# Attention and two feed-forward layers on one core: the first layer's hidden chunks are handled two at a time in one PSUM bank

## The chip, the cores and the metric

One core of a Trainium2 chip runs the whole program. The metric is the device time of one execution in microseconds (us). The kernel before was run three times: 1081.27, 1083.11 and 1083.59 us, median 1083.11 us.

## The reference, cut to what matters

```python
# 4 batches, 8 heads, 576 positions, head size 64
scores = q @ k.T / 8 + (cum[:, :, :, None] - cum[:, :, None, :])   # cum: running sum of log f
attn = softmax(where(causal, -1e9, scores)) @ v
x = attn as 2304 tokens x 512
h = x @ w_in                    # 512 -> 2048
g = h * clip(h + 3, 0, 6) / 6   # first layer
x = g @ w_out                   # 2048 -> 512
h = x @ w2_in                   # second layer, other weights
g = where(h >= 1, h, where(h <= -1, 0, (h + 1)**2 / 4))
out = g @ w2_out
```

## The kernel before

Tokens are the free axis. The first layer goes over nine blocks of 256 tokens (`NB`, `T`), the second over blocks of 512, 512, 512, 512 and 256 (`T2`). The 2048 hidden features are cut into 16 chunks of 128 (`NCH`). One entry of `steps` is one block and one chunk, (j, n, c): 144 entries for the first layer, 80 for the second. Each product of two fp32 numbers is made of three matmuls, since every operand is held as a rounded part and a rest: high by high, low by high, high by low.

`moe_h(g)` makes the features of one entry: 12 matmuls (4 slices of 128 inputs, 3 each) into one PSUM bank `hp`. In the first layer these have 256 columns. Then come four elementwise instructions on 256 columns: ScalarE (ACT) Relu out of `hp` into `u` (L567), VectorE (DVE) minimum and product with `hp` (L568), ACT rounding of `u` into the high half of `g` (helper L121), DVE subtraction into its low half (helper L129). `moe_o(g)` multiplies `g` with the second weights: 12 matmuls that add to the block's accumulators. In the first layer these are two banks, each holding two slices of 256 columns (L608); since two slices share a bank, a block begins with two matmuls of a zero row, one per bank, that set the bank to zero (L601). In the second layer the matmuls have 512 columns, three in a row for each group of 128 tokens (L615), with (weight part a, feature part bb) in the order (0,0), (1,0), (0,1).

Order of the work. The main loop takes one entry g per turn: weights due for g (`weights_until`), `moe_h(g)`, attention pieces, `moe_o(g - 2)` (`LAG` is 2), attention pieces again. Attention pieces (scores, softmax, transposes, products with v) are taken from a list `seq`, so many at each point that running costs meet a goal (`goal`, `due`). They share TensorE (PE), ACT, DVE and the four PSUM banks of `ps` (later two more) with the first layer, and are all done by entry 112 (`g7`). In the first 32 entries blocks 0 and 1 alternate, block 1 being `STAG` = 9 chunks behind. Weights live in 12 slots of 8 KB per partition (16 from entry 112 on). `plan_weights` decides which chunk sits where, and counts a slot as free `LAG` + 1 entries after its last use. The tile framework then sets the final order on each engine by a simulated schedule, so an engine's instructions need not come in the order in which the loop writes them. All loads are issued from SyncE's queue (SP), each in its turn.

Of the kernel before, what the change touches and what calls it, by code (L numbers as in the profile page):

```python
# [8 lines left out]
F32 = mybir.dt.float32  # L9
F32R = mybir.dt.float32r  # L10
I32 = mybir.dt.int32
AF = mybir.ActivationFunctionType
# [4 lines left out]
P = 128  # L17
NCH = DFF // P
KD = DM // P
T = 256  # L20
# [16 lines left out]

SLOTS = 12
MORE = 16 - SLOTS
LAG = 2  # L40
STAG = 9
XT = 11
PRE0, PRE1 = 38, 106
WRAW = 4
# [30 lines left out]
def tile_kernel(  # L75
# [38 lines left out]
    ncum = dram.tile([B * H, S], F32, name="ncum")  # L114
    wsb = [wpool.tile([P, 2, 8, P], F32R, name=f"w{s}") for s in range(SLOTS)]
    ident = const.tile([P, P], F32, name="ident")
    zero = const.tile([1, P], F32R, name="zero")

    def rounded(eng, out, in_):
        if eng == "a":  # L120
# [9 lines left out]


    steps = []
    for i in range(NCH + STAG):
        if i < NCH:
            steps.append((0, i, i))
        if i >= STAG:
            steps.append((1, i - STAG, i - STAG))
    for j in range(2, NB2):
        order = range(NCH) if j % 2 else range(NCH - 1, -1, -1)
        for n, c in enumerate(order):  # L140
# [58 lines left out]
    def w_keep(c, s):  # L199
        nc.sync.dma_start(out=wf[c], in_=wsb[s].bitcast(F32))  # L200
# [339 lines left out]
    def moe_x(j):  # L540

        t0, w = sum(T2[:j - NB]), T2[j - NB]
        for k in range(KD):
            x = ext.tile([P, 2, T2[0]], F32R, tag=f"x2{k}", name=f"x2{k}", bufs=2)
            hi, lo = x[:, 0, 0:w], x[:, 1, 0:w]
            nc.sync.dma_start(out=lo.bitcast(F32), in_=x2d[k * P:(k + 1) * P, t0:t0 + w])
            rounded("p", hi, lo.bitcast(F32))
            rest("v", lo, lo.bitcast(F32), hi)
            xt[j, k] = x

    def moe_h(g):
        j, n, c = steps[g]
        layer = int(j >= NB)
        w = T2[j - NB] if layer else T
        ws = wsb[where[g]]
        hp = bank("hp")
        hp = hp[:, 0:w]
        for k in range(KD):
            x = xt[j, k]
            for a, bb in ((0, 0), (1, 0), (0, 1)):  # L560
                nc.tensor.matmul(  # L561
                    hp, lhsT=ws[:, a, k], rhs=x[:, bb, 0:w], start=(k == 0 and a == 0 and bb == 0),
                    stop=(k == KD - 1 and bb == 1),
                )
        u = ffn.tile([P, T2[0] if layer else T], F32, tag="u", name="u", bufs=2)[:, 0:w]
        if layer == 0:
            nc.scalar.activation(out=u, in_=hp, func=AF.Relu, bias=3.0, scale=1.0)  # L567
            nc.vector.scalar_tensor_tensor(out=u, in0=u, scalar=6.0, in1=hp, op0=ALU.min, op1=ALU.mult)  # L568
        else:
            nc.scalar.activation(out=u, in_=hp, func=AF.Relu, bias=0.5, scale=0.5)  # L570
            nc.scalar.activation(out=u, in_=u, func=AF.Square)  # L571
            nc.vector.scalar_tensor_tensor(out=u, in0=hp, scalar=1.0, in1=u, op0=ALU.max, op1=ALU.min)  # L572
        gg = ffn.tile([P, 2, T2[0] if layer else T], F32R, tag="g", name="g", bufs=3)[:, :, 0:w]
        rounded("a", gg[:, 0], u)
        rest("v", gg[:, 1], u, gg[:, 0])
        gt[g] = gg
# [10 lines left out]
    def moe_o(g):  # L587
        j, n, c = steps[g]
        layer = int(j >= NB)
        t0 = sum(T2[:j - NB]) if layer else j * T  # L590
        ws = wsb[where[g]]
        gg = gt.pop(g)
        if n == 0:
            acc[j] = [(ps_x if j == 1 else ps_o).tile([P, 512], F32, tag=f"o{k}", name=f"o{k}") for k in range(2)]
            if layer:
                acc[j] += [ps_b[0].tile([P, 512], F32, tag="ps", name="ps") for _ in range(T2[j - NB] // P - 2)]
        if layer == 0:

            if n == 0:
                for k in range(2):  # L600
                    nc.tensor.matmul(  # L601
                        acc[j][k].rearrange("p (a n) -> p a n", a=4), lhsT=zero,
                        rhs=zero.unsqueeze(1).to_broadcast([1, 4, P]), start=True, stop=False,
                    )
            for k in range(KD):
                o = acc[j][k // 2][:, k % 2 * T:k % 2 * T + T]
                for a, bb in ((0, 0), (1, 0), (0, 1)):
                    nc.tensor.matmul(  # L608
                        o, lhsT=ws[:, a, KD + k], rhs=gg[:, bb], start=False,
                        stop=(n == NCH - 1 and bb == 1 and k % 2 == 1),  # L610
                    )
        else:
            for k in range(len(acc[j])):
                for a, bb in ((0, 0), (1, 0), (0, 1)):
                    nc.tensor.matmul(  # L615
                        acc[j][k], lhsT=gg[:, bb, k * P:(k + 1) * P],
                        rhs=ws[:, a, KD:2 * KD].rearrange("p k n -> p (k n)"),
                        start=(n == 0 and a == 0 and bb == 0), stop=(n == NCH - 1 and bb == 1),
                    )
# [104 lines left out]
    nc.vector.tensor_scalar(out=lf0, in0=lf0, scalar1=-8.0, scalar2=None, op0=ALU.mult)  # L724
    nc.sync.dma_start(out=lf, in_=f.rearrange("b h (g l) -> (b h g) l", g=SEG))
    make_identity(nc, ident)
    zf = att.tile([P, P], F32, tag="prob0", name="zf")
    nc.vector.memset(zf[0:1], 0.0)
    nc.vector.tensor_copy(zero, zf[0:1])
    logs(lf)  # L730
    seq, ends = attention_pieces()
    u_load(0)
# [22 lines left out]
        weights_until(-1)  # L755


    spans = [(0, STAG, 1), (STAG, 2 * NCH, 2)] + [(j * NCH, (j + 1) * NCH, j + 1) for j in range(2, NB)]
    cost = [sum(x[0] for x in seq[:n]) for n in range(len(seq) + 1)]
    due = [ends[group(min(j, NB - 1))] for _, _, j in spans]  # L760
    goal, n0 = [], pos
# [10 lines left out]
            n0 += 1  # L772

    ext = None
    for g in range(len(steps) + LAG):
        if g == g7:
            assert pos == len(seq)
            att_cm.__exit__(None, None, None)
            ext = ctx.enter_context(tc.tile_pool(name="ext", bufs=2, reuse_waits="tile"))
            wsb += [ext.tile([P, 2, 8, P], F32R, name=f"w{s}", bufs=1) for s in range(SLOTS, SLOTS + MORE)]  # L780
        weights_until(g)
        if g < n1:
            for part in range(2):
                if part == 0:
                    moe_h(g)
                elif g >= LAG:
                    moe_o(g - LAG)
                    j, n, c = steps[g - LAG]
                    if j == 0 and again[c]:
                        w_keep(c, where[g - LAG])  # L790
                while pos < len(seq) and cost[pos] < goal[2 * g + part] - 1:
                    seq[pos][1]()
                    pos += 1
            if g == 2 * NCH + LAG - 1:
                psx_cm.__exit__(None, None, None)
                ps_b.append(ctx.enter_context(
                    tc.tile_pool(name="ps_b", bufs=2, space=bass.MemoryType.PSUM, reuse_waits="tile")
                ))
            if g == g7 + 20:
                moe_x(NB)  # L800
            if g == n1 - 1:
                moe1_cm.__exit__(None, None, None)
                ffn = ctx.enter_context(tc.tile_pool(name="moe2", bufs=2, side="right", reuse_waits="tile"))
        else:
            second[0] = True
            if g < len(steps):
                j, n, c = steps[g]
                moe_h(g)
                if n == 4 and j + 1 < NB2:
                    moe_x(j + 1)  # L810
            moe_o(g - LAG)


# [36 lines left out]
```

## Time and profile before

| | |
|---|---|
| runs | 1081.27, 1083.11, 1083.59 us |
| profiled execution: span from first to last instruction | 1083.4 us |
| PE busy | 1034.3 us, 95% |
| PE weight loads busy | 903.9 us, 83% |
| DVE busy | 591.8 us, 55% |
| ACT busy | 541.5 us, 50% |
| matmuls | 6556 |

The page gives no time for the profiled execution other than its span, which lies inside the three runs. Busy PE is modelled from pipelined matmuls, so its share is not a share of peak; the starts of successive matmuls tell the pace.

### The profile page before, as it was taken

The numbers are of one execution on the slowest core, as the hardware profiler recorded it, in microseconds if no ns is written. First come the engines' busy times: TensorE is split into PE (matmuls) and PEld (weight loads), VectorE is DVE, ScalarE is ACT, GpSimd is POOL, SyncE is SP. The second block draws the span as 40 slices with busy tenths as digits, with TensorE's granted clock in tenths as the row PEclk, the third lists the DMA queues.
The fourth block names the chain that finished last, engine by engine and source line by source line (L and its number), as shares of the span: only waits on it lengthen the run. The fifth ranks groups of instructions, "written<-read, shape, count | busy, mean of one in ns | idle before, by whom it ended". The sixth has DMA issues, their size and how long they took to land.

```text
span 1083.4 us, 18101 instructions
## 1 busy us (share of the span) xinstructions
PE 1034.3 (95%) x6556; PEld 903.9 (83%) x6556; DVE 591.8 (55%) x1510; ACT 541.5 (50%) x1330; POOL 89.8 (8%) x223
## 2 busy tenths in 40 slices
PE   7987999989799989999999999999999999999998
PEld 5776989979688889888989999888888888888887
DVE  7999984766577776777653436422422322332232
ACT  6877755656456655556553235533333333333343
POOL 2200010111021111121101000000100100000000
PEclk8688999999999999999999999999999999999999
DMA  8976681783586686864826035200200200010010
GB/s 235 337 222 185 213 299 54 226 277 111 182 282 197 202 298 185 282 212 123 249 68 253 2 96 167 90 1 1 77 1 1 72 6 1 19 39 1 1 40 20
DMA packets 69785, 144.20 MB, mean 133 GB/s; under 512 B 11584, under 2 KB 38720, under 8 KB 65600
## 3 DMA queue, kind: packets, MB, share of 16 engines
q1 hardware_dynamic: 67136, 134.66, 39.6%
q0 software_dynamic: 2560, 8.39, 2.0%
q8 instruction: 51, 0.84, 0.3%
q14 instruction: 38, 0.31, 0.1%
HBM read 116.74 MB, written 26.29 MB: 132 GB/s over the span
## 4 chain that ended last, share of the span: by engine, by line
PE 69%; DMA 15%; DVE 7%; issue 4%; ACT 4%; SPq 1%; POOL 0%; DVEq 0%; ACTq 0%; POOLq 0%
PE hp L561 31%; PE o L608 12%; PE o L615 10%; PE ps L615 8%; DMA qraw<-in_q 5%; DMA dec<-ncum 3%; PE pt L432 3%; DMA kraw<-in_k 2%; PE av L474 2%; DMA wraw<-in_w 2%; PE sc L388 1%; DMA x2d<-osb 1%; DMA wf<-wr 1%; DVE prob L339 1%; DVE wr L186 1%
## 5 line engine op out<-in xcount | busy, mean ns | idle before, releaser
L608 PE MATMUL o<-g,w 128*128 128x256 f32 x1728 | 250.3, 289 | 16.8 <-ACT g L121 15.3
L561 PE MATMUL hp<-xt,w 128*128 128x256 f32 x1728 | 250.6, 292 | 7.8 <-ACT w L121 5.1
L608 PEld LDWEIGHTS o<-g,w 128*128 128x128 f32 x1728 | 225.9, 191 | 26.7 <-ACT g L121 19.2
L561 PEld LDWEIGHTS hp<-xt,w 128*128 128x128 f32 x1728 | 226.8, 194 | 14.5 <-ACT w L121 6.1
L561 PE MATMUL hp<-x,w 128*128 128x512 f32 (+1 forms) x960 | 211.4, 369 | 0.0
L561 PEld LDWEIGHTS hp<-x,w 128*128 128x128 f32 x960 | 169.1, 188 | 32.5
L572 DVE SCALAR_TENSOR_TENSOR u<-hp,u 128x512 f32<-128x512 f32 (+1 forms) x80 | 50.8, 637 | 195.9 <-ACT u L571 195.9
L129 DVE TENSOR_TENSOR g<-u,g 128x256 fp32r<-128x256 f32 (+1 forms) x224 | 112.8, 505 | 71.5 <-ACT g L121 71.1
L121 ACT ACTIVATE g<-u 128x256 fp32r<-128x256 f32 (+1 forms) x224 | 106.1, 475 | 88.4 <-DVE u L572 55.3
L570 ACT ACTIVATE u<-hp 128x512 f32<-128x512 f32 (+1 forms) x80 | 44.6, 557 | 173.3 <-PE hp L561 171.5
L615 PE MATMUL o<-w,g 128*128 128x512 f32 x480 | 125.0, 396 | 0.0
L615 PEld LDWEIGHTS o<-w,g 128*128 128x128 f32 x480 | 89.1, 188 | 19.9
L345 ACT ACTIVATE prob<-prob,mx 128x512 f32<-128x512 f32 (+4 forms) x144 | 83.5, 581 | 37.4 <-DVE mx L339 37.0
L615 PE MATMUL ps<-w,g 128*128 128x512 f32 x384 | 100.4, 396 | 0.0
L568 DVE SCALAR_TENSOR_TENSOR u<-u,hp 128x256 f32<-128x256 f32 x144 | 59.4, 416 | 53.8 <-ACT u L567 53.2
L567 ACT ACTIVATE u<-hp 128x256 f32<-128x256 f32 x144 | 53.8, 378 | 67.2 <-PE hp L561 65.4
L615 PEld LDWEIGHTS ps<-w,g 128*128 128x128 f32 x384 | 72.3, 188 | 17.4
L432 PE MATMUL pt<-ident,prob 128*128 128x128 f32 (+1 forms) x400 | 69.1, 296 | 12.6 <-DVE prob L417 12.1
L339 DVE CUSTOM_DVE_ANT_0 prob<-sc,dec 128x256 f32<-128x256 f32 (+1 forms) x112 | 58.8, 533 | 25.1 <-PE sc L388 11.9
L121 ACT ACTIVATE pt<-pt 128x512 f32<-128x512 f32 (+3 forms) x160 | 61.9, 433 | 18.7 <-PE pt L432 18.2
L432 PEld LDWEIGHTS pt<-ident,prob 128*128 128x128 f32 (+1 forms) x400 | 50.3, 150 | 18.4 <-DVE prob L417 12.8
L178 ACT ACTIVATE wr<-wraw 128x512 f32<-128x512 f32 x64 | 43.0, 671 | 44.5 <-DMA wf<-wr 19.0
(76 smaller groups left out, 975.5 us busy)
## 6 DMA issues: line engine op xcount, KB each, us to landing
wraw<-in_w SPq DMA_DIRECT2D x64, 512.0 KB, 6.4
w<-wf SPq DMA_DIRECT2D x24, 1024.0 KB, 8.5
dec<-ncum SPq DMA_DIRECT2D x45, 256.0 KB, 6.6
kraw<-in_k SPq DMA_DIRECT2D x64, 144.0 KB, 3.8
wf<-w SPq DMA_DIRECT2D x8, 1024.0 KB
wf<-wr POOLq DMA_DIRECT2D x32, 256.0 KB, 6.0
w<-wf SPq DMA_DIRECT2D x16, 512.0 KB, 4.1
vv<-in_v SPq DMA_DIRECT2D x16, 320.0 KB, 10.6
```

The source lines that it names most:

```text
L121: nc.scalar.activation(out=out, in_=in_, func=AF.Copy)
L129: e.tensor_tensor(out=out, in0=in_, in1=hi.bitcast(F32), op=ALU.subtract)
L339: nc.vector.tensor_tensor_reduce(out=py[:, a:e], in0=s, in1=dc, scale=-0.125, scalar=mx[:, 2 * z:2 * z + 1] if x else 3.0e38, op0=ALU.add, ...
L345: nc.scalar.activation(out=py, in_=py, func=AF.Exp, scale=-1.0, bias=mx[:, 2 * z + x:2 * z + x + 1], accum_out=sm[:, z:z + 1],)
L432: nc.tensor.transpose(t[:nk, o:o + P], p[:, c:c + nk], ident)
L561: nc.tensor.matmul(hp, lhsT=ws[:, a, k], rhs=x[:, bb, 0:w], start=(k == 0 and a == 0 and bb == 0), stop=(k == KD - 1 and bb == 1),)
L567: nc.scalar.activation(out=u, in_=hp, func=AF.Relu, bias=3.0, scale=1.0)
L568: nc.vector.scalar_tensor_tensor(out=u, in0=u, scalar=6.0, in1=hp, op0=ALU.min, op1=ALU.mult)
L570: nc.scalar.activation(out=u, in_=hp, func=AF.Relu, bias=0.5, scale=0.5)
L572: nc.vector.scalar_tensor_tensor(out=u, in0=hp, scalar=1.0, in1=u, op0=ALU.max, op1=ALU.min)
L608: nc.tensor.matmul(o, lhsT=ws[:, a, KD + k], rhs=gg[:, bb], start=False, stop=(n == NCH - 1 and bb == 1 and k % 2 == 1),)
L615: nc.tensor.matmul(acc[j][k], lhsT=gg[:, bb, k * P:(k + 1) * P], rhs=ws[:, a, KD:2 * KD].rearrange("p k n -> p (k n)"), start=(n == 0 and ...
```

## The change

- First layer: chunks go in pairs. The second chunk of a pair writes columns 256 to 511 of the bank that the first one began; only then come the four elementwise instructions, on 512 columns. `u` has one buffer of twice the size in place of two, `g` two of twice the size in place of three.
- The loop takes two entries per turn: features of both (attention pieces after each), then the output products of the pair before (pieces after each). The planner's `LAG` is 3, and `LAG2` = 2 is the distance in the second layer. Blocks 0 and 1 alternate by pairs, `STAG` = 8; block 1 begins at entry 10 in both kernels.
- No zero matmuls: the first matmul into each accumulator bank carries the start flag. The zero tile and the two instructions that make it go.
- Second layer: the three matmuls of the output product come in the order (0,0), (0,1), (1,0).

```diff
-LAG = 2
-STAG = 9
+LAG = 3
+LAG2 = 2
+STAG = 8
...
-    for i in range(NCH + STAG):
+    for i in range(0, NCH + STAG, 2):
         if i < NCH:
-            steps.append((0, i, i))
+            steps += [(0, i, i), (0, i + 1, i + 1)]
         if i >= STAG:
-            steps.append((1, i - STAG, i - STAG))
+            steps += [(1, i - STAG, i - STAG), (1, i + 1 - STAG, i + 1 - STAG)]
...
-        hp = bank("hp")
-        hp = hp[:, 0:w]
+        first = layer or g % 2 == 0
+        if first:
+            half["hp"] = bank("hp")
+        bk = half["hp"]
+        hp = bk[:, 0:w] if first else bk[:, w:2 * w]
...
         if layer == 0:
+            if first:
+                return
+            hp = bk[:, 0:2 * T]
+            u = ffn.tile([P, 2 * T], F32, tag="u", name="u", bufs=1)
             nc.scalar.activation(out=u, in_=hp, func=AF.Relu, bias=3.0, scale=1.0)
             nc.vector.scalar_tensor_tensor(out=u, in0=u, scalar=6.0, in1=hp, op0=ALU.min, op1=ALU.mult)
...
+            gg = ffn.tile([P, 2, 2, T], F32R, tag="g", name="g", bufs=2)
+            hi, lo = (gg[:, x].rearrange("p c n -> p (c n)") for x in range(2))
+            rounded("a", hi, u)
+            rest("v", lo, u, hi)
+            gt[g - 1], gt[g] = gg[:, :, 0], gg[:, :, 1]
+            return
...
-            if n == 0:
-                for k in range(2):
-                    nc.tensor.matmul(
-                        acc[j][k].rearrange("p (a n) -> p a n", a=4), lhsT=zero,
-                        rhs=zero.unsqueeze(1).to_broadcast([1, 4, P]), start=True, stop=False,
-                    )
...
-                        o, lhsT=ws[:, a, KD + k], rhs=gg[:, bb], start=False,
+                        o, lhsT=ws[:, a, KD + k], rhs=gg[:, bb], start=(n == 0 and k % 2 == 0 and a == 0 and bb == 0),
...
-                for a, bb in ((0, 0), (1, 0), (0, 1)):
+                for a, bb in ((0, 0), (0, 1), (1, 0)):
...
+    for g in range(0, n1, 2):
...
+        for x in range(2):
+            weights_until(g + x)
+            moe_h(g + x)
+            pieces(2 * g + x)
+        for x in range(2):
+            y = g - 2 + x
+            if y >= 0:
+                moe_o(y)
...
+            pieces(2 * g + 2 + x)
...
+    for g in range(n1, len(steps) + LAG2):
```

## Rows read from the trace of the kernel before

**Rows 1.** The page: busy time of each engine, then the span in 40 slices.
```profile
PE 1034.3 (95%) x6556; PEld 903.9 (83%) x6556; DVE 591.8 (55%) x1510; ACT 541.5 (50%) x1330; POOL 89.8 (8%) x223
...
PE   7987999989799989999999999999999999999998
```

**Rows 2.** Busy time by stage: each window's length, each engine's busy us, PEclk, DMA.
```profile
45.00:590.00 545.00, 508.69 (x3855) 461.73 (x3853) 390.65 (x1118) 326.52 (x908) 70.33 (x182) 0.97 0.66 209
590.00:673.40 83.40, 83.40 (x682) 82.10 (x682) 39.70 (x74) 31.35 (x67) 3.22 (x6) 1.00 0.30 90
673.40:1083.40 410.00, 405.47 (x1871) 334.87 (x1869) 124.24 (x192) 150.36 (x260) 7.52 (x12) 1.00 0.08 26
```

**Rows 3.** Who waited for whom, 45 to 590 us: total us, times, longest.
```profile
ACT wr L178 <- DMA wf<-wr: 19.0, 7, 6.6
...
PE o L608 <- ACT g L121: 15.3, 11, 2.8
...
PE pt L432 <- DVE prob L417: 10.2, 6, 3.6
```

**Rows 4.** Timeline of a stage without attention: start, us, engine, instructions.
```profile
619.95 1.60 PE L561 MATMUL hp<-xt,w 128*128 128x256 f32 x12
...
621.64 0.39 ACT L567 ACTIVATE u<-hp 128x256 f32<-128x256 f32 x1 [1.59 <-PE hp L561]
...
622.83 1.60 PE L561 MATMUL hp<-xt,w 128*128 128x256 f32 x12
622.97 0.42 DVE L129 TENSOR_TENSOR g<-u,g 128x256 fp32r<-128x256 f32 x1 [0.48 <-ACT g L121]
```

**Rows 5.** PE timeline at the start of the last block of the first layer.
```profile
637.07 0.49 PE L601 MATMUL o<-zero 1*128 1x512 f32 x1
637.49 0.62 PE L608 MATMUL o<-g,w 128*128 128x256 f32 x3
...
638.46 1.35 PE L608 MATMUL o<-g,w 128*128 128x256 f32 x9
```

**Rows 6.** Groups by line and shape: count, busy us, mean ns, idle before.
```profile
L601 PE MATMUL o<-zero 1*128 1x512 f32 x18 | 8.5, 520 | 1.5 <-DVE zero L729 1.5
...
L567 ACT ACTIVATE u<-hp 128x256 f32<-128x256 f32 x144 | 53.8, 378 | 67.2 <-PE hp L561 65.4 <-DVE wr L183 0.9 <-DVE g L129 0.7
L568 DVE SCALAR_TENSOR_TENSOR u<-u,hp 128x256 f32<-128x256 f32 x144 | 59.4, 416 | 53.8 <-ACT u L567 53.2
L121 ACT ACTIVATE g<-u 128x256 fp32r<-128x256 f32 x160 | 65.7, 413 | 39.2 <-DVE u L568 31.3 <-DVE u L572 7.4
L129 DVE TENSOR_TENSOR g<-u,g 128x256 fp32r<-128x256 f32 x160 | 68.6, 430 | 30.8 <-ACT g L121 30.5
L570 ACT ACTIVATE u<-hp 128x512 f32<-128x512 f32 x64 | 38.4, 600 | 154.8 <-PE hp L561 153.0 <-DVE g L129 1.7
L572 DVE SCALAR_TENSOR_TENSOR u<-hp,u 128x512 f32<-128x512 f32 x64 | 44.0, 690 | 174.0 <-ACT u L571 174.0
L121 ACT ACTIVATE g<-u 128x512 fp32r<-128x512 f32 x64 | 40.3, 632 | 49.2 <-DVE u L572 47.9 <-PE ps L615 1.2
L129 DVE TENSOR_TENSOR g<-u,g 128x512 fp32r<-128x512 f32 x64 | 44.2, 692 | 40.7 <-ACT g L121 40.6
```

**Rows 7.** Timeline around the longest wait of an output product for its features.
```profile
222.38 0.66 ACT L178 ACTIVATE wr<-wraw 128x512 f32<-128x512 f32 x1 [6.57 <-DMA wf<-wr]
...
224.15 0.50 PE L608 MATMUL o<-g,w 128*128 128x256 f32 x2 [2.78 <-ACT g L121]
```

**Rows 8.** PE timeline of one step of the second layer.
```profile
850.52 2.90 PE L561 MATMUL hp<-x,w 128*128 128x512 f32 x12
853.25 1.56 PE L615 MATMUL o<-w,g 128*128 128x512 f32 x6
...
856.06 2.90 PE L561 MATMUL hp<-x,w 128*128 128x512 f32 x12
```

**Rows 9.** The page: DMA issues of the weight reloads, KB each, us to landing.
```profile
w<-wf SPq DMA_DIRECT2D x24, 1024.0 KB, 8.5
```

More of the change, by code (lines that the diff above doesn't have):

```diff
@@ L116, in tile_kernel @@
     ident = const.tile([P, P], F32, name="ident")
-    zero = const.tile([1, P], F32R, name="zero")
     def rounded(eng, out, in_):
@@ L549, in moe_x @@
             xt[j, k] = x
+    half = {}
     def moe_h(g):
@@ L561, in moe_h @@
                 nc.tensor.matmul(
-                    hp, lhsT=ws[:, a, k], rhs=x[:, bb, 0:w], start=(k == 0 and a == 0 and bb == 0),
-                    stop=(k == KD - 1 and bb == 1),
+                    hp, lhsT=ws[:, a, k], rhs=x[:, bb, 0:w], start=(first and k == 0 and a == 0 and bb == 0),
+                    stop=((layer or not first) and k == KD - 1 and bb == 1),
                 )
-        u = ffn.tile([P, T2[0] if layer else T], F32, tag="u", name="u", bufs=2)[:, 0:w]
         if layer == 0:
+            if first:
+                return
+            hp = bk[:, 0:2 * T]
+            u = ffn.tile([P, 2 * T], F32, tag="u", name="u", bufs=1)
             nc.scalar.activation(out=u, in_=hp, func=AF.Relu, bias=3.0, scale=1.0)
             nc.vector.scalar_tensor_tensor(out=u, in0=u, scalar=6.0, in1=hp, op0=ALU.min, op1=ALU.mult)
[L569 to L573, printed above, removed]
+            gg = ffn.tile([P, 2, 2, T], F32R, tag="g", name="g", bufs=2)
[4 more added lines that the diff above has]
+            return
+        u = ffn.tile([P, T2[0]], F32, tag="u", name="u", bufs=2)[:, 0:w]
+        nc.scalar.activation(out=u, in_=hp, func=AF.Relu, bias=0.5, scale=0.5)
+        nc.scalar.activation(out=u, in_=u, func=AF.Square)
+        nc.vector.scalar_tensor_tensor(out=u, in0=hp, scalar=1.0, in1=u, op0=ALU.max, op1=ALU.min)
+        gg = ffn.tile([P, 2, T2[0]], F32R, tag="g", name="g", bufs=3)[:, :, 0:w]
         rounded("a", gg[:, 0], u)
@@ L617, in moe_o @@
                         rhs=ws[:, a, KD:2 * KD].rearrange("p k n -> p (k n)"),
-                        start=(n == 0 and a == 0 and bb == 0), stop=(n == NCH - 1 and bb == 1),
+                        start=(n == 0 and a == 0 and bb == 0), stop=(n == NCH - 1 and a == 1),
                     )
@@ L726, in tile_kernel @@
     make_identity(nc, ident)
-    zf = att.tile([P, P], F32, tag="prob0", name="zf")
-    nc.vector.memset(zf[0:1], 0.0)
-    nc.vector.tensor_copy(zero, zf[0:1])
     logs(lf)
@@ L755, in tile_kernel @@
         weights_until(-1)
-    spans = [(0, STAG, 1), (STAG, 2 * NCH, 2)] + [(j * NCH, (j + 1) * NCH, j + 1) for j in range(2, NB)]
+    spans = [(0, STAG + 1, 1), (STAG + 1, 2 * NCH, 2)] + [(j * NCH, (j + 1) * NCH, j + 1) for j in range(2, NB)]
     cost = [sum(x[0] for x in seq[:n]) for n in range(len(seq) + 1)]
@@ L774, in tile_kernel, with pieces @@
     ext = None
-    for g in range(len(steps) + LAG):
+    def pieces(x):
+        nonlocal pos
+        while pos < len(seq) and cost[pos] < goal[x] - 1:
+            seq[pos][1]()
+            pos += 1
+    for g in range(0, n1, 2):
         if g == g7:
@@ L780, in tile_kernel @@
             wsb += [ext.tile([P, 2, 8, P], F32R, name=f"w{s}", bufs=1) for s in range(SLOTS, SLOTS + MORE)]
-        weights_until(g)
[L782 to L811, printed above, removed]
@@ new lines, in tile_kernel @@
+        for x in range(2):
[6 more added lines that the diff above has]
+                moe_o(y)
+                j, n, c = steps[y]
+                if j == 0 and again[c]:
+                    w_keep(c, where[y])
+            pieces(2 * g + 2 + x)
+        if g == 2 * NCH:
+            psx_cm.__exit__(None, None, None)
+            ps_b.append(ctx.enter_context(
+                tc.tile_pool(name="ps_b", bufs=2, space=bass.MemoryType.PSUM, reuse_waits="tile")
+            ))
@@ L815 @@
+        if g == g7 + 20:
+            moe_x(NB)
+    moe1_cm.__exit__(None, None, None)
+    ffn = ctx.enter_context(tc.tile_pool(name="moe2", bufs=2, side="right", reuse_waits="tile"))
+    second[0] = True
+    for g in range(n1, len(steps) + LAG2):
+        weights_until(g)
+        if g < len(steps):
+            j, n, c = steps[g]
+            moe_h(g)
+            if n == 4 and j + 1 < NB2:
+                moe_x(j + 1)
+        moe_o(g - LAG2)
 def kernel(**inputs):
```

## The prediction

> **What bounds the kernel now.** The page's busy times come first, with the slices beside them: PE is busy for 1034.3 us of a span of 1083.4, and full in nearly every slice from the middle on, while DVE and ACT are at half [rows 1]. So PE sets the end, and the question is where it works on something that can go, and where it stands. The table by stage answers the second part [rows 2]. From 45 to 590 us, where attention and the first layer share the engines, PE stands 545 - 508.7 = 36.3 us, DVE is busy 390.7 of 545 us (72%), and the granted clock is 0.97. From 590 to 673 PE does not stand at all. From 673 on, in the second layer, the rows lack 4.5 us at the drained end and nothing before it. The first 45 us belong to attention's start and to weight loads, which the change leaves alone.
>
> The waits of the middle stage tell what PE stands for [rows 3]: 15.3 us, in 11 places, until ACT has made the high part of `g`; 10.2 us until DVE has scaled attention's probabilities. The largest of the first kind shows the root [rows 7]: ACT stood 6.57 us at L178 for a weight store to land, everything behind it in ACT's queue came late, and the output product began after 2.78 us of standing. All such stores together hold ACT for 19.0 us [rows 3], and the change does not touch them.
>
> Without attention the pace is plain [rows 4]: `hp` starts at 619.95 and again at 622.83, so one entry costs 2.88 us, its 24 matmuls 0.12 us each. The elementwise chain runs from 621.64 to 623.39 and its product is due two entries later, so nothing waits.
>
> The span and the median of the runs (1083.11) differ by 0.3 us; I sum against 1083.1. About 0.2%, 2.2 us, can be told from no change.
>
> **Zero matmuls.** They go, 18 of them, two for each of nine blocks [rows 6]. What one costs is read from starts, not from its 520 ns, which contain the drain [rows 5]. The first starts at 637.07 and the next product at 637.49: 0.42 us. Three matmuls of 0.12 us take PE to 637.85, and the product behind the second zero matmul starts at 638.46: 0.61 us. Mean 0.51. The four of blocks 0 and 1 lie where PE waits for loads: nothing. The other 14 make 14 x 0.51 = 7.1 us. Six of them (the last three blocks) stand where PE hardly ever waits and are gained whole, 3.1 us. Of the other eight, 4.1 us, a part only lengthens the next wait; PE stands 7% of that stage, but waits come in clumps, so I take 60%, 2.4 us. Sum -5.5; ends -7.1 and -3.1. What replaces them is a flag. A block's first product still waits until the block before is copied out of the bank; that wait stays, and behind a pair's `hp` there are now 24 matmuls to cover it in place of 12.
>
> **Elementwise work at 512 columns.** Rows for 256 against rows for 512 [rows 6]; for Relu and the product with `hp` the nearest 512-column rows are the second layer's, which also read one PSUM and one SBUF operand or just PSUM. ACT per pair: 2 x (378 + 413) = 1582 ns becomes 600 + 632 = 1232, 350 less. DVE: 2 x (416 + 430) = 1692 becomes 690 + 692 = 1382, 310 less. Over 72 pairs that is 25.2 us of ACT and 22.3 of DVE; 56 pairs, 17.4 us of DVE, lie ahead of entry 112, in the stage where engines are shared. Neither engine is the bound, so little of it comes through: where PE stands for attention's results or for `g`, these queues are shorter by 17.4 of 390.7 us, 4.5%, but a good part of the standing is a DMA's doing, as in rows 7. The ends are 0 and 17.4 us. Less standing also keeps the clock up: 0.97 in this stage is a mean of two levels, full and half, so about 6% of it, 33 us, ran at half and cost some 16 us beside 36.3 us of standing. I take -5.
>
> **The wait that is added.** The first chunk's features now wait for the second chunk: 12 more matmuls, 1.44 us, and the pieces between. Then the chain of four takes 600 + 690 + 632 + 692 = 2614 ns in place of 378 + 416 + 413 + 430 = 1637, 0.98 us longer. Its product is due behind the other pair's 24 output matmuls and the next pair's 24 feature matmuls, 5.76 us; before, four groups of 12 also made 5.76 us. So a chain has about 3 us to spare in place of 4, with no attention piece counted, and in the stage from 590 us on the cost is nothing. In the middle stage, where a store holds ACT, a late chain is later by 0.98 us, and what is queued behind its four instructions (probabilities, `pt`, the next `g`) moves with it. Against this there are half as many chains to be late. With 11 waits: half of them would give back 7.7 us, and 11 each longer by 0.98 would cost 10.8. I take 0, near the middle, with -7.7 and +10.8 as ends.
>
> The PSUM side of it: a bank is held from the first chunk's first matmul to the end of the product with `hp`. Before, two banks were held for 1.44 us plus their Relu and product, 2.2 us each; now one for 2.88 + 1.29 us plus the pieces between. That is 4.2 against 4.5 bank-us, so attention's pieces have as many banks: nothing. That the first half could be read while the second is written, and the chain of chunk one start early, is excluded by the Trainium skill, "PSUM — Partial Sum Buffer", section "PSUM bank collisions raise a hardware error": two engines may not touch one bank in the same partitions at once. Rows 4 fit it only in that Relu comes after all 12 matmuls of its bank; no row shows a read of half a bank. If the halves could be split, the added 1.44 us would go, and by the sum above nothing more.
>
> **Weights and the planner.** With `LAG` 3 a slot is free one entry later. Working `plan_weights` through for both kernels gives 56 loads each, the same chunks in the same order, with 8 entries in place of 9 between a free slot and its next use for 20 of the 24 reloads; four get slots from the new pool. Eight entries are 8 x 2.88 = 23 us, a reload lands in 8.5 [rows 9]: nothing. On SP's queue a load now stands behind output products that are at least as old as before, so what waits behind it there (loads of q, k and `ncum`) is not held longer. Attention pieces keep four places per pair and their goals: nothing, though the simulated schedule may order them otherwise; that is in the range, 4 us either way.
>
> **Second layer.** Feature matmuls run at (853.25 - 850.52) / 12 = 0.2275 us, output products at (856.06 - 853.25) / 12 = 0.2342 [rows 8]. The products load the same weights twice in a row; feature matmuls never do. The new order ends this. If that is the cause, 2.81 - 2.73 = 0.08 us per step of 512 columns and chunk, 864 products in all, gives -5.8 us. Were the reverse true, the cost is bounded by the same 5.8. The order changes neither columns nor counts, so I take 0.
>
> **Sum.** -5.5 - 5 + 0 + 0 + 0 = -10.5: 1083.1 - 10.5 = 1072.6, say 1072.5.
>
> **Rivals.** (A) Only the zero matmuls count, and half of what elementwise work frees is lost again: -3.1 to -5.5, about 1079. For it: ACT and DVE are not the bound, and DMA ends the waits. Against it: DVE is at 72% where PE stands. (B) The second layer takes its new order at the feature matmuls' pace: 1072.5 - 5.8 = 1066.7. For it: the one difference in weights that I can name. Against it: the starts of products within a step show no period of three. (C) Slower: the longer chain. In the middle stage `g` is late at 11 places and, with a spare of 3 us in place of 4, at 6 more. Eleven at 0.98 plus six at a mean wait of 15.3 / 11 = 1.4 us are 19.2 us; less 5.5 for zero matmuls and nothing for freed engines, 1083.1 + 13.7 = 1096.8. It decides against me once the added waits exceed 10.5 us. For it: the store waits of rows 3 and 7. Against it: half as many chains. (D) The change does not do what it says: the schedule moves attention so that what is freed returns as standing elsewhere, 1083 within 2 us.
>
> **How the numbers follow.** Forecast (1062 to 1077) 0.47, A 0.15, B 0.14, C 0.14, D 0.10. The predicted time is 1072.5. The range reaches down past B, to all ends that are likely together, 1057, and up past D to 1085.5; C is left out above it. Faster: forecast, A and B, less a little of A that falls inside 2.2 us, 0.73. Same: D and that little, 0.12. Slower: C and a little, 0.15.
>
> **What would show it.** No L601 rows; in the second half, blocks begin without a pause. Relu rows of 512 columns near 600 ns, the product near 690, 72 each, and DVE's busy time in all near 570, ACT's near 516. PE's standing from 45 us to the last attention piece below 36 us, at a clock of 0.97 or more. A second layer of 410 us if the order is nothing, 404 if B holds. I am wrong if `PE o` waits for ACT's `g` add up to much more than 15.3 us, if PE waits for a PSUM bank inside a pair, or if the second layer's pace moves up.

## The result, and the profile after

The changed kernel takes 1100.23 us, the median of 4 runs (1094.03 to 1103.09); the kernel before, beside it, 1082.80 (1081.27 to 1083.59). The ratio is 1.0143, 95% interval [1.0119, 1.0168]: 1.4% slower, outside the predicted range of 1057 to 1085.5. The profiled execution took 1094.03 us, the shortest of the four, with a span of 1092.3. Its rows are read against [rows 1 to 9], whose span is 1083.4. The spans differ by 8.9 us, so the rows show about half of the 17.4 us that separate the medians. (The time of an execution is 1.7 us longer than its span here, 1094.03 against 1092.3; by that the profiled execution before took an estimated 1085.1 us, which lies above its three runs and not inside them.)

First the page: busy time of each engine, then the span in 40 slices.

```profile
PE 1023.7 (94%) x6538; PEld 900.3 (82%) x6538; DVE 580.1 (53%) x1364; ACT 526.5 (48%) x1186; POOL 95.2 (9%) x223
...
PE   6877889899888999889999999999999999999998
```

All three busy times fell against [rows 1], and the span grew: the loss is standing. Twelve of the first 18 slices are below nine, where six were. The table by stage (busy us of PE, PEld, DVE, ACT, POOL, then the granted clock and the DMA share) says where.

```profile
45.00:590.00 545.00, 491.26 (x3727) 449.55 (x3728) 376.95 (x992) 309.81 (x781) 72.69 (x178) 0.95 0.63 198
590.00:682.30 92.30, 92.30 (x771) 91.06 (x770) 40.01 (x54) 31.39 (x47) 5.28 (x8) 1.00 0.41 139
682.30:1092.30 410.00, 405.76 (x1874) 335.52 (x1872) 124.11 (x190) 150.06 (x258) 7.50 (x12) 1.00 0.08 25
```

In the stage where attention and the first layer share the engines PE stands 545 - 491.26 = 53.7 us, against 36.3 in [rows 2], and the granted clock is 0.95 in place of 0.97. The last attention product starts at 593.4 us; before, at 580.7: 12.7 us later. The rest of the first layer then takes less: from there to its last output product 100.06 us in place of 103.51. Of these 3.45 us some 2.47 are four zero matmuls that are gone (the first experiment), and the rest is eight matmuls at 0.12 us that were done earlier. What follows takes 398.90 us in place of 399.19. 12.69 - 3.45 - 0.29 = 8.95, which is what the span grew by. Entry 32 starts at 190.2 us, and at 190.9 before: up to there nothing is lost.

Who waited, from 45 to 600 us (total, times, longest):

```profile
PE o L617 <- ACT g L121: 25.8, 9, 5.5
...
ACT wr L178 <- DMA wf<-wr: 22.1, 6, 8.5
...
PE pt L432 <- DVE prob L417: 13.9, 5, 7.8
```

The same names as in [rows 3], each with more time in fewer places: `PE o` for `g` waits 2.9 us a time (25.8 / 9) where it waited 1.4 (15.3 / 11). A few long stalls make the difference. Counted over the trace, PE stood over 3 us at a time twice from 45 to 600 us before, 7.0 us in all, and six times after, 28.9 us in all. The longest of them, in the timeline (start, us, engine, instructions, in brackets the idle time before and what ended it; `wr` holds a half of a weight chunk until it is stored to `wf` in memory, `dec` is attention's copy of the running sums `ncum`):

```profile
454.74 0.24 POOL L302 TENSOR_SCALAR_AFFINE_SELECT dm<-dec 128x64 f32<-128x64 f32 x1 [12.39 <-DMA dec<-ncum]
455.05 0.23 POOL L306 TENSOR_SCALAR_AFFINE_SELECT dm<-dec 64x64 f32<-64x64 f32 x1
455.53 1.09 POOL L194 DMA_DIRECT2D wf<-wr  x2 [0.25 <-issue]
...
458.13 3.04 PE L617 MATMUL o<-g,w 128*128 128x256 f32 x24
...
462.18 0.66 ACT L178 ACTIVATE wr<-wraw 128x512 f32<-128x512 f32 x1 [8.48 <-DMA wf<-wr]
...
465.12 0.72 ACT L345 ACTIVATE prob<-prob,mx 128x512 f32<-128x512 f32 x1 [0.95 <-DVE mx L339]
...
468.58 0.63 ACT L121 ACTIVATE g<-u 128x512 fp32r<-128x512 f32 x1 [0.47 <-DVE u L577]
...
469.02 0.66 PE L432 MATMUL pt<-ident,prob 128*128 128x128 f32 x2 [7.85 <-DVE prob L417]
```

Read it from the bottom. PE ended its 24 output products at 461.17 and stood 7.85 us until probabilities were scaled. Those came late because ACT had stood 8.48 us at L178, with softmax and the next `g` behind it in its queue. L178 needs a `wr` buffer, free when a weight store has landed; that store was issued at 455.53 and landed at 462.15; it was issued so late, with a second one, because POOL, which issues it, had itself waited 12.39 us for a load of `dec`. Nothing in this chain was edited. The kernel before has the same chain at the same place, in a milder order:

```profile
448.32 0.23 POOL L302 TENSOR_SCALAR_AFFINE_SELECT dm<-dec 128x64 f32<-128x64 f32 x1 [9.17 <-DMA dec<-ncum]
448.62 0.23 POOL L306 TENSOR_SCALAR_AFFINE_SELECT dm<-dec 64x64 f32<-64x64 f32 x1
449.10 0.56 POOL L194 DMA_DIRECT2D wf<-wr  x1 [0.24 <-DVE u L568]
...
455.58 0.66 ACT L178 ACTIVATE wr<-wraw 128x512 f32<-128x512 f32 x1 [5.16 <-DMA wf<-wr]
...
457.54 0.54 PE L432 MATMUL pt<-ident,prob 128*128 128x128 f32 x2 [2.70 <-DVE prob L417]
```

There PE stood 2.70 us. What each engine has queued behind such a wait is settled when the program is built: its scheduler simulates a timeline and fixes every engine's order by it. The written order of the change goes into that simulation, and another order of everything comes out.

What the edited lines cost, in groups by shape:

```profile
L129 DVE TENSOR_TENSOR g<-u,g 128x512 fp32r<-128x512 f32 x136 | 93.8, 691 | 58.9 <-ACT g L121 58.0
L121 ACT ACTIVATE g<-u 128x512 fp32r<-128x512 f32 x136 | 85.5, 629 | 77.4 <-DVE u L587 47.9 <-DVE u L577 25.9 <-PE ps L624 3.3
L577 DVE SCALAR_TENSOR_TENSOR u<-u,hp 128x512 f32<-128x512 f32 x72 | 49.3, 684 | 53.0 <-ACT u L576 52.8
...
L576 ACT ACTIVATE u<-hp 128x512 f32<-128x512 f32 x72 | 42.5, 590 | 57.7 <-PE hp L566 57.0 <-DVE g L129 0.6
```

They answer to [rows 6], and each duration is within 10 ns of the one taken from there. And the stage without attention, where nothing waits:

```profile
641.97 3.04 PE L617 MATMUL o<-g,w 128*128 128x256 f32 x24
642.17 0.60 ACT L576 ACTIVATE u<-hp 128x512 f32<-128x512 f32 x1 [3.77 <-PE hp L566]
...
644.85 3.04 PE L566 MATMUL hp<-xt,w 128*128 128x256 f32 x24
...
647.73 3.04 PE L617 MATMUL o<-g,w 128*128 128x256 f32 x24
```

A pair costs 647.73 - 641.97 = 5.76 us, twice the 2.88 of [rows 4].

### The profile page after: what moved, and what is told of

It is laid out like the page before. It is cut to its first block, busy times and chain, and to the rows that moved or that the text cites. A ratio compares the mean times of both kernels' runs of the same rounds, so it can differ in the third digit from the quotient of the medians.

```text
span 1092.3 us, 17702 instructions
## 1 busy us (share of the span) xinstructions
PE 1023.7 (94%) x6538; PEld 900.3 (82%) x6538; DVE 580.1 (53%) x1364; ACT 526.5 (48%) x1186; POOL 95.2 (9%) x223
## 4 chain that ended last, share of the span: by engine, by line
PE 68%; DMA 15%; DVE 9%; issue 4%; ACT 3%; SPq 1%; POOL 0%; DVEq 0%; POOLq 0%; ACTq 0%
PE hp L566 29%; PE o L617 13%; PE o L624 10%; PE ps L624 8%; DMA kraw<-in_k 5%; DMA dec<-ncum 4%; PE pt L432 2%; PE av L474 2%; DMA qraw<-in_q 2%; DMA wf<-wr 2%; DVE prob L339 2%; PE sc L388 2%; DVE wr L186 1%; DVE kk L129 1%; DVE wr L189 1%
## 5 line engine op out<-in xcount | busy, mean ns | idle before, releaser
L617 PE MATMUL o<-g,w 128*128 128x256 f32 x1728 | 243.9, 291 | 28.6 <-ACT g L121 25.8
L566 PE MATMUL hp<-xt,w 128*128 128x256 f32 x1728 | 240.9, 290 | 3.5 <-ACT w L121 2.4
L566 PEld LDWEIGHTS hp<-xt,w 128*128 128x128 f32 x1728 | 222.6, 193 | 8.7 <-ACT w L121 2.8
L129 DVE TENSOR_TENSOR g<-u,g 128x512 fp32r<-128x512 f32 (+1 forms) x152 | 100.6, 663 | 66.7 <-ACT g L121 65.9
L121 ACT ACTIVATE g<-u 128x512 fp32r<-128x512 f32 (+1 forms) x152 | 92.2, 607 | 84.8 <-DVE u L587 55.3
L339 DVE CUSTOM_DVE_ANT_0 prob<-sc,dec 128x256 f32<-128x256 f32 (+1 forms) x112 | 58.8, 534 | 43.5 <-PE sc L388 25.2
L432 PE MATMUL pt<-ident,prob 128*128 128x128 f32 (+1 forms) x400 | 66.2, 289 | 16.6 <-DVE prob L417 16.5
L577 DVE SCALAR_TENSOR_TENSOR u<-u,hp 128x512 f32<-128x512 f32 x72 | 49.3, 684 | 53.0 <-ACT u L576 52.8
L576 ACT ACTIVATE u<-hp 128x512 f32<-128x512 f32 x72 | 42.5, 590 | 57.7 <-PE hp L566 57.0
L178 ACT ACTIVATE wr<-wraw 128x512 f32<-128x512 f32 x64 | 43.0, 673 | 45.2 <-DMA wf<-wr 22.1
```

Source lines behind the costliest of these rows:

```text
L121: nc.scalar.activation(out=out, in_=in_, func=AF.Copy)
L129: e.tensor_tensor(out=out, in0=in_, in1=hi.bitcast(F32), op=ALU.subtract)
L178: nc.scalar.activation(out=rf, in_=hw.bitcast(F32), func=AF.Abs)
L339: nc.vector.tensor_tensor_reduce(out=py[:, a:e], in0=s, in1=dc, scale=-0.125, scalar=mx[:, 2 * z:2 * z + 1] if x else 3.0e38, op0=ALU.add, ...
L432: nc.tensor.transpose(t[:nk, o:o + P], p[:, c:c + nk], ident)
L566: nc.tensor.matmul(hp, lhsT=ws[:, a, k], rhs=x[:, bb, 0:w], start=(first and k == 0 and a == 0 and bb == 0), stop=((layer or not first) an ...
```

## The experiments

Each ratio is to the kernel before, run on the same chip in the same rounds, with a 95% interval. "Standing" is 545 us less PE's busy time in the window from 45 to 590 us, in the profiled execution. The two theories that lived to the end: **theory 1**, the pair form costs something of its own; **theory 5**, the forms are equal in the mean, and what moves the time is which order of instructions the scheduler's simulated timeline happens to give. The others were about single parts of the form: the later chain, the longer chain, the bank held longer, the distance to the product. In the first expectations theory 1 still names the merged chain as what costs; theory 6 is ACT's wait for the weight stores.

**Zero matmuls alone.** The kernel before, without them.

```diff
-            if n == 0:
-                for k in range(2):
-                    nc.tensor.matmul(
-                        acc[j][k].rearrange("p (a n) -> p a n", a=4), lhsT=zero,
...
-                        o, lhsT=ws[:, a, KD + k], rhs=gg[:, bb], start=False,
+                        o, lhsT=ws[:, a, KD + k], rhs=gg[:, bb], start=(n == 0 and k % 2 == 0 and a == 0 and bb == 0),
```

> The kernel before, without its zero matmuls alone. By my sum the 14 zero matmuls behind the start are worth 3.1 to 7.1 us: 1077 us. Both theories of the slowdown (the longer chain of the merged instructions; the order of two features, then two products) say the same here. If it is 1083 or more, the zero matmuls cost nothing where they stood.

Measured: 1.000 [0.9986, 1.0015]. From the last attention product to the last output product of the first layer PE runs the same 819 matmuls in both traces, but for four zero matmuls that lie there before:

```profile
589.77 0.49 PE L601 MATMUL o<-zero 1*128 1x512 f32 x1
...
590.74 0.49 PE L601 MATMUL o<-zero 1*128 1x512 f32 x1
...
637.07 0.49 PE L601 MATMUL o<-zero 1*128 1x512 f32 x1
...
638.04 0.49 PE L601 MATMUL o<-zero 1*128 1x512 f32 x1
```

Without them it takes 101.05 us in place of 103.51: 2.47 us, 0.62 for each. Ahead of that the last attention product starts 1.7 us later, at 582.4, and PE stands 545 - 503.11 = 41.9 us, 5.6 more than before. Eleven zero matmuls were in that window, by their mean of 0.47 us (8.5 / 18 [rows 6]) an estimated 5.2 us that counted as busy: about what they left came back as standing.

```profile
45.00:590.00 545.00, 503.11 (x3830) 456.88 (x3830) 390.94 (x1117) 324.61 (x904) 71.16 (x180) 0.97 0.67 208
```

**Pair order without merging.** The changed kernel with a bank and a chain of 256 columns for each chunk; then the same with both chains held back until the second chunk's features are done, the added wait without the merged instructions.

```diff
-        first = layer or g % 2 == 0
+        first = True
...
-            u = ffn.tile([P, 2 * T], F32, tag="u", name="u", bufs=1)
+            u = ffn.tile([P, T], F32, tag="u", name="u", bufs=2)
```

To the second kernel this is added:

```diff
+            half[g] = hp
+            if g % 2 == 0:
+                return
+            for y in (g - 1, g):
+                hp = half.pop(y)
```

> The changed kernel with the pair order of the loop kept, but each chunk with its own bank and its own four instructions on 256 columns. Theory 1 (the merged chain, longer and begun later, makes g late): the loss goes, about 1077 us. Theory 2 (the pair order itself costs it, whatever the size of the instructions): stays at about 1100 us.

> Pair order with 256-column instructions and a bank for each chunk (0.9988 of the kernel before when each chain started with its own chunk), but both chunks' chains are issued only behind the second chunk's matmuls. Theory 1a (what hurts is that the first chunk's chain starts late, so that two chunks' elementwise work comes in one burst with the pair's products due behind it): 1.008 to 1.018 of the kernel before, near the changed kernel. Theory 1b (what hurts is the size of the single instructions): stays within 0.996 to 1.002.

Measured: 0.9988 [0.9974, 1.0001], and with the wait 0.9994 [0.998, 1.0007]. In the first the loss goes, as theory 1 has it, but to 1083.77 us and not to 1077; the second fits theory 1b. In these two orders neither the pair order nor the wait for the second chunk costs anything that shows.

**Merging without pair order.** One bank and a 512-column chain for two chunks, but features and products alternate, each product three entries behind.

```diff
-    for g in range(0, n1, 2):
+    for g in range(n1):
...
-        for x in range(2):
-            weights_until(g + x)
-            moe_h(g + x)
-            pieces(2 * g + x)
-        for x in range(2):
-            y = g - 2 + x
+        weights_until(g)
+        moe_h(g)
+        pieces(2 * g)
+        for y in [g - 3] + [g - 2] * (g == n1 - 1):
...
```

> The changed kernel with the merged instructions on 512 columns kept, but features and products alternating one entry at a time, the product of a chunk three entries behind. Theory 1 (merged chain): stays at about 1100 us. Theory 2 (pair order): the loss goes, about 1077 us.

Measured: 0.9932 [0.9915, 0.9948], 1078.35 us, faster than both kernels, with the same merged chain, the same added wait and a bank held longer. So none of these three costs 1.4% wherever it is used. One order does not speak for a whole form, here and above, as the disturbances show further down.

**No attention pieces inside a pair, and a longer spare.** First both pieces of a pair's features are put behind the second chunk, so the bank and the chain wait for no piece. Then, from entry 32 on, products come two pairs behind and the rounding of `g` stands behind them, so that a late chain has a whole pair more before it is missed (the slots of the weights are planned for the longer distance).

```diff
             moe_h(g + x)
-            pieces(2 * g + x)
+        pieces(2 * g)
+        pieces(2 * g + 1)
```
```diff
-            y = g - 2 + x
+            y = g - (2 if near else 4) + x
...
+            if x == 1 and not near:
+                moe_g(g + 1)
...
```

> The changed kernel with no attention pieces between the two feature chunks of a pair; they come behind the second. Theory 3 (the bank that is held open across attention pieces, and the later start of the chain that goes with it, is the loss): 1085 to 1090 us. Theories 1 and 2: about 1100 us as before.

> The changed kernel, but from entry 32 on a pair's products come two pairs behind its features in place of one, and the rounding into g is issued behind the products that free its buffer. Theory 1 (late chains make PE wait): most of the loss goes, 0.985 to 0.998 of the kernel before. Theory 4 (the order in which the simulated schedule lays attention between pairs is the loss, and the distance is not): 1.010 to 1.018 as the changed kernel.

Measured: 1.0114 [1.0088, 1.0141] and 1.018 [1.0162, 1.0197]. The first mends at most a little. The second should have mended most if `g` came late by a microsecond or two for want of spare; it is the slowest of its kind, PE stands 545 - 486.33 = 58.7 us in it, and eight stalls of over 3 us make 35.1 of that. Three of the eight lie ahead of entry 32, at 192.6 us, where the distance is the old one. From there on PE's waits of `o` for ACT's `g` are 11.1 us, and 11.4 in the changed kernel: the longer spare did not shorten them. This speaks against the longer chain as a cause (rival C), in one order.

**A disturbance that changes no work.** Attention pieces are written until their planned cost is within one unit of the goal of the place; here they stop 300, 600 or 1000 units short of it. No instruction is added or removed; some pieces are written at a later place. In the traces every engine runs the same set of instructions as without it, in another order: at 300, 1878 of PE's 6538 matmuls stand at another place in the changed kernel, 1997 in the old form (the kernel before without zero matmuls).

```diff
-        while pos < len(seq) and cost[pos] < goal[x] - 1:
+        while pos < len(seq) and cost[pos] < goal[x] - 300:
```

On the changed kernel:

> A control for the scatter of schedules: the changed kernel with attention's goals met 300 cost units earlier or later by rounding (a piece is held back when the goal is less than 300 away, in place of 1). If the pair with the merged chain is slow by its structure: 1.009 to 1.019 of the kernel before. If the changed kernel is slow by the luck of one schedule: anywhere from 0.990 to 1.015.

> The changed kernel whole, with one number changed: an attention piece is held back if its goal is less than 600 units of its planner's cost ahead, in place of 1. No operation is added or taken away; only the written place of a few pieces moves. Theory 5 (forms are equal in the mean, each drawn schedule lies anywhere from 0.993 to 1.018): a new draw, not bound to the 1.0143 of the changed kernel; most likely 0.997 to 1.008. Theory 1 (the pair form with merged instructions has a cost of its own of about 1%): 1.008 or more.

> Second draw of a schedule for the changed kernel: pieces held back when the goal is less than 1000 cost units away. Theory 5 (the pair form is worth about as much as the kernel before, and one schedule of it lies anywhere within some 1.5%): 0.990 to 1.015 of the kernel before. Theory 1 (its structure costs 1.4%, and the run with 300 was a lucky one): 1.009 to 1.019.

On the kernel before without zero matmuls, and on the merged chain in alternating order:

> The same disturbance on the kernel before without zero matmuls (1.000 undisturbed). Theory 5a (every form scatters alike): as far as 1% from 1.000. Theory 5b (merged chains scatter more, since a chain that comes late delays 24 products and has a microsecond less to spare): 0.997 to 1.003, as all four 256-column schedules measured so far.

> The kernel before without its zero matmuls, threshold 600 units in place of 1: the partner of the changed kernel with 600 (1.0031). If forms are equal in the mean (theory 5): anywhere from 0.989 to 1.018, above 1.0031 as likely as below it. If the pair form with merged instructions costs about 0.6 to 1% of its own, as four of the five pairs so far say: 0.993 to 0.998.

> The kernel before without its zero matmuls, with the threshold at 1000 units in place of 1, the disturbance that took the changed kernel from 1.0143 to 0.9974. Theory 5: a new draw of the old form, 0.993 to 1.018, not bound to its 1.000. Theory 1: the old form stays at 1.000 within 0.003; then the 1.0111 at 300 units would be the odd one out.

> The same control for the merged chain with alternating features and products (0.9932 of the kernel before). Structure: 0.989 to 0.998. Luck of the schedule: anywhere from 0.990 to 1.015.

Measured: the changed kernel 1.0003 [0.9991, 1.0016], 1.0031 [1.0012, 1.005] and 0.9974 [0.9957, 0.999]; the old form 1.0111 [1.0096, 1.0125], 1.0022 [1.0006, 1.0039] and 0.9895 [0.9866, 0.9924]; the alternating merged form 1.001 [0.9992, 1.0028]. PE's waits of `o` for ACT's `g` in the three, at 300, 600 and 1000:

```profile
PE o L617 <- ACT g L121: 17.7, 9, 4.1
PE o L617 <- ACT g L121: 17.3, 6, 8.4
PE o L617 <- ACT g L121: 17.2, 7, 4.9
```

The chain is as long there as in the changed kernel, and the waits are near the 15.3 us of [rows 3] in place of 25.8: the longer chain as a cause of the 1.4% (rival C) falls here. The whole loss goes when pieces are written at slightly other places, and the old form loses nearly as much by the same means, or gains 1% of it. The old form at 300 shows the signature of the changed kernel, without any part of the change but the missing zero matmuls. Its stage from 45 to 590 us:

```profile
45.00:590.00 545.00, 491.28 (x3730) 449.13 (x3726) 386.21 (x1107) 320.96 (x892) 70.66 (x178) 0.95 0.64 198
```

PE stands 53.7 us at a clock of 0.95, the changed kernel's numbers. The longest stall has the same root too:

```profile
215.84 0.23 POOL L301 TENSOR_SCALAR_AFFINE_SELECT dm<-dec 128x64 f32<-128x64 f32 x1 [11.73 <-DMA dec<-ncum]
...
216.38 1.10 POOL L193 DMA_DIRECT2D wf<-wr  x2
...
222.80 0.66 ACT L177 ACTIVATE wr<-wraw 128x512 f32<-128x512 f32 x1 [8.98 <-DMA wf<-wr]
...
227.62 0.69 PE L431 MATMUL pt<-ident,prob 128*128 128x128 f32 x2 [8.70 <-DVE prob L416]
```

POOL waits for `dec`, two stores go out together behind it, ACT waits 8.98 us for the first to land, and PE stands 8.70. The same form at 1000 has one stall of over 3 us in place of five (6.3 us in place of 26.8), stands 35.1 us at 0.97, and its 1073.22 us is the lowest median of all:

```profile
45.00:590.00 545.00, 509.86 (x3913) 465.63 (x3914) 396.50 (x1126) 329.69 (x912) 70.47 (x186) 0.97 0.67 210
```

**A third buffer for the stored weights,** so that L178 meets a landed store more often. In the changed kernel the scratch tile `upper` moves to the pool of `g` to make room.

```diff
-        r = moe.tile([P, 4, P], F32, tag="wr", name="wr", bufs=2)
+        r = moe.tile([P, 4, P], F32, tag="wr", name="wr", bufs=3)
...
-    upper = att.tile([P, QA], F32, tag="upper", name="upper", bufs=1)
+    upper = moe1.tile([P, 2, 2, T], F32, tag="g", name="upper", bufs=2)[:, 0, 0]
```

> The changed kernel with three in place of two buffers for the weight halves that wait for their store (wr), so that ACT stands less at that load; one constant moves to another pool to make room. Theory 6 (the loss is ACT held by those stores, 22.1 us in all and at each of the three longest PE waits, which the merged chain passes on to PE): 0.985 to 1.000 of the kernel before, and the wait of wr for the store below 8 us. If the loss is elsewhere: 1.005 to 1.018.

> The same three buffers on the kernel before without zero matmuls, which also waits 20.3 us for those stores. Theory 6: 0.990 to 0.999, a smaller gain than in the changed kernel, since the 256-column chain has more to spare. If those waits are hidden there: 0.998 to 1.002.

Measured: 1.0043 [1.0029, 1.0057] and, on the old form, 0.9974 [0.9962, 0.9986]. Both fall, by 1.0 and 0.3%, and the first misses theory 6's 0.985 to 1.000. But ACT's wait for stores falls less than the time in the changed kernel, from 22.1 to 18.7 us in all, and the longest is still 9.0 where theory 6 had it below 8, so most of the gain is again another order. That the buffer itself helps is likely from the mechanism and not shown apart from the draw.

**Without the simulated timeline.** The same written kernels, put in order by the framework's plain scheduler.

```diff
-    with tile.TileContext(nc, schedule_with_timeline_sim=True) as tc:
+    with tile.TileContext(nc) as tc:
```

> The changed kernel whole, written order untouched, but the instructions are put in order by the framework's plain scheduler in place of the one that simulates a timeline. If the order drawn by the simulated timeline makes the loss, this kernel and the old form under the same plain scheduler (the other run of this pair) differ by less than 0.5%, at whatever level the plain order gives (0.99 to 1.05 of the kernel before). If the form has a cost of its own, this one is about 1% above the other.

> The kernel before without its zero matmuls, under the plain scheduler. It is the base for the changed kernel under the same scheduler: equal to it within 0.5% if the loss is one of drawn order, about 1% below it if the pair form costs of itself. Against the kernel before: 0.99 to 1.05; the simulated order may be worth something by itself.

> The form with merged 512-column instructions, but features and products of single chunks alternating, no zero matmuls, under the plain scheduler. If the 1% between the two forms under that scheduler (1.0452 for pairs with merged instructions against 1.0348 for single chunks) comes from merging the chain, this one is at 1.045; if it comes from the pair order of features and products, at 1.035; below 1.030 the merged chain is a gain and the pair order costs more than 1%.

Measured: pairs 1.0452 [1.0422, 1.0481], the old form 1.0348 [1.0318, 1.0378], merged and alternating 1.03 [1.0283, 1.0318]. The simulated timeline is worth 3 to 4% to all of them. Between pairs and the old form 1% remains, against what theory 5 expected, and pairs lie 1.5% above the alternating form with the same merged chain, so under this scheduler the pair order goes with the slower time and the merging does not. PE's waits for the scaled probabilities differ most, from 45 to 627 us 57.2 us in the pair form

```profile
PE pt L432 <- DVE prob L417: 57.2, 17, 7.1
```

and 33.1 in the old form (whether they are the cause was not tested):

```profile
PE pt L431 <- DVE prob L416: 33.1, 12, 7.3
```

**All draws together,** as ratios to the kernel before:

| | old form, no zero matmuls | merged, alternating | merged pairs (the change) |
|---|---|---|---|
| threshold 1 | 1.000 | 0.9932 | 1.0143 |
| threshold 300 | 1.0111 | 1.001 | 1.0003 |
| threshold 600 | 1.0022 | | 1.0031 |
| threshold 1000 | 0.9895 | | 0.9974 |
| third `wr` buffer | 0.9974 | | 1.0043 |
| plain scheduler | 1.0348 | 1.03 | 1.0452 |

Merged pairs less the old form, row by row, in per cent: +1.43, -1.08, +0.09, +0.79, +0.69, +1.04. The rows are one kernel pair each. The mean is +0.5 and, taken as six draws, its 95% interval -0.4 to +1.4. Theory 5 holds for the scatter: within one form and the simulated timeline the ratio moves over 2.2% (0.9895 to 1.0111) and 1.7% (0.9974 to 1.0143). Not all of it need be chance: at 1000 both forms are at their lowest, so that the later place may itself be worth something; two kernels cannot tell. A profile shows one of a kernel's executions: that of the changed kernel at 1000 took 1088.65 us where the median is 1081.63, so the verdicts rest on the ratios and not on the spans. The same scatter limits every single run above, and the kernel before, with its zero matmuls, was itself built in one order alone. Whether the pair form costs half a per cent of its own besides is open; five of six rows are above zero, and the interval holds zero. Merging in alternating order, with products three entries behind, is below the old form in all three rows (-0.68, -1.01, -0.48; mean -0.7, interval -1.4 to -0.1).

## Why the prediction was wrong

**The step that failed** is the one on weights and the planner: "Attention pieces keep four places per pair and their goals: nothing, though the simulated schedule may order them otherwise; that is in the range, 4 us either way." Its size was off. The same operations with pieces written a little elsewhere lay from 0.9895 to 1.0111 in the old form, about 12 us either way. That term is larger than the whole forecast of -10.5 and stands ahead of every other. Rival D came nearest in kind, the schedule as the cause, but it let the schedule only take a gain away, not add a loss. The forecast gain does not show in the mean either: the four thresholds of the changed form average 1.0038 of the kernel before, those of the old form 1.0007, where -10.5 us would be 0.990.

**Zero matmuls.** The price was a little low where PE never waits: 0.62 us each by four of them, where starts had said 0.51. The other two of my six lie ahead of the last attention product, at 518.80 and 520.46; PE hardly waits there, but no run shows their worth apart. In the shared stage I took 60% of 4.1 us; no run shows that either, because the order is drawn anew when they go, and in the one order without them nothing was gained (1.000).

**Elementwise work.** The durations were right (684 ns for 690, 590 for 600), the busy time was not: DVE lost 11.7 us (591.8 to 580.1) where I said 22.3, ACT 15.0 where I said 25.2. The summed durations did fall nearly as forecast, by 20.4 us on DVE. But an instruction often starts before the one ahead of it has ended: before, DVE's durations sum to 671.2 us and cover 591.8, after, 650.8 and 580.1. I read the zero matmul from starts for that reason, and did not do so here. That the freed time then comes through as 5 us cannot be told from the scatter; merging in alternating order points to some 8 us (0.7% of 1083), with an interval from 1 to 15.

**The added wait.** Nothing that shows beside the scatter, as predicted: 0.9994 with the wait and without merging, 0.9932 with both. The measured waits of `PE o` for `g` did grow well past 15.3 us, the sign that I had named for being wrong, but by long stalls in 9 places and not by 0.98 us in each. Rival C's time (1096.8) is near the measured one and its mechanism is not the cause: with the chain just as long, other orders have 17.2 to 17.7 us of these waits and no such loss. The rule of the Trainium skill, "PSUM — Partial Sum Buffer", section "PSUM bank collisions raise a hardware error", that two engines may not be in one bank and the same partitions at once, fits the rows after: the Relu of a pair starts at 642.17, when the second chunk's features have ended. No run reads half a bank while the other half is written.

**The second layer.** 410.0 us before and after, as forecast. From the first layer's last output product on it takes 398.90 us in place of 399.19, so the order of the three products is worth at most 0.3 us, and rival B with its 5.8 is out.

## What to carry to other kernels

Where a scheduler fixes the order from a simulated timeline, one timing of an edit is one draw: disturb the order in both versions without changing the work, and compare the sets before believing a change of a per cent. Read the long stalls first, and follow each one back past the engine that the wait names, here from PE over DVE and ACT to a store and to the queue that issues it. Take what a merge saves from start to start, not from durations, which overlap.

## What the runs showed of the hardware

Back-to-back instructions on VectorE overlap in the profile: in the kernel before 995 of 1510 started before the one ahead of them had ended, and 79 us of durations (671.2 - 591.8) were covered twice, 0.08 us for each of the 995. Four zero matmuls (one row, 512 columns, each opening a bank) in a stretch where PE never waited cost 2.47 us, 0.62 each, where starts had said 0.42 to 0.61. And the granted clock in the stage from 45 to 590 us went with the standing only roughly: 0.97 at 35.1 us (the old form at 1000) and at 36.3 (before), 0.95 at 53.7 (the changed kernel), 0.94 at 58.7 (products two pairs behind); but 0.97 as well at 45.6 (pair order without merging) and 0.95 at 42.6 (the changed kernel with a third `wr` buffer), so the total alone doesn't set it.
